# A decay attention with gated convolution on one Trainium2 core: another order of all pieces, and fixed buffer places

## The chip, the core and the metric

The kernel runs on one core of one Trainium2 chip. The metric is the time of one execution on the device, in microseconds (us); lower is better. A core has TensorE (PE, with its weight loads, PEld), VectorE (DVE), ScalarE (ACT), GpSimd (POOL) and SyncE (SP, which here issues all the DMAs). Each engine works through its own instructions in order; they meet at semaphores.

## What is computed

Two layers in a row, in float32, for 4 sequences of 768 tokens, 8 heads of 64 columns. The first is attention with an exponential decay per head, in blocks with a running state; the second gates its output with the sigmoid of a causal convolution over 5 tokens and projects twice:

```python
intra = np.einsum('bhic,bhjc->bhij', qb, kb) * Dmask[None]
intra = np.einsum('bhij,bhjd->bhid', intra, vb)
inter = np.einsum('bhid,bhde->bhie', qb * lam_pow[None], kv_state)
out[:, :, sl] = intra + inter
kb_dec = kb * rev_pow[None]
kv_state = lam_block * kv_state + np.einsum('bhsd,bhse->bhde', kb_dec, vb)
# second layer, x is the attention's output with the heads side by side
gate_pre += conv_w[k][None, None, :] * xp[:, k:k + S, :]      # k = 0..4
gate = 1.0 / (1.0 + np.exp(-gate_pre))
return (gate * (x @ w_val)) @ w_out
```

The weights `w_val`, `conv_w` and `w_out` come as float64, the rest as float32.

## The kernel before

The work is cut into 12 items: a pair of sequences times six chunks of 128 tokens. Items 0 to 5 belong to the first pair, 6 to 11 to the second. All work is a list of 695 named pieces, each with an engine, the pieces it needs, and a function that emits its instructions; `plan.add` collects them. A table, `ORDER`, lists all names once. `Plan.run` (line 101) walks the table and emits each piece, so a piece stands on its engine in the order of the table. No scheduler changes that.

The pieces, with i the item, b the sequence of the pair, u a half of the columns or heads:

- SP: `ld.i.0` and `ld.i.2` load the two halves (1 MB each) of an item; `wv.u`, `wo.u` load halves of the two weights (1 MB each), `cv` the convolution's; `o.i.b.j` stores.
- Weights: `wv.u.k.*`, `wo.u.k.*`, `cv.*` make float32 out of the float64 bits: `e`, `w`, `s`, `v` on VectorE (lines 241 to 270), `m`, `r` on ScalarE; then `h` rounds to a high part on ScalarE (276) and `l` subtracts to a low part on POOL (280). `dm`, `dc`, `qe` make the decay masks.
- Attention on TensorE: `s` scores (431, 441; items 0 to 2 are done in "big" form, whole chunks of 128, in two halves), `ia` scores times v (496, 481), `in` the state's part (507, 518), `st` the state's update (535, 543). Around it: `m` masks on VectorE (454, 461), `up` adds the state there (550, 552), `fd` fades it on POOL (555), `kd` scales k on ScalarE or POOL (378, 381), `qd` scales q on POOL (390, 397).
- Between the layers: `x` copies the result for the convolution (605), `hi` its history, `xh` and `xl` split it into a high part (ScalarE, 627, 629) and a low part (`x_lo`; VectorE for items 0 and 1, 635, else POOL, 639).
- Second layer: `v.i.f` is a quarter of x @ w_val (line 704, twelve matmuls of 256 columns: high by high, low by high, high by low); `t.n.c.k` are the five taps (663 on ScalarE, 665 on VectorE), `sg` the sigmoid, for units of two items; `pb` copies v out of PSUM for items 0 to 5, `ap` gates (718), `hh` and `hl` split again (741, 744); `p.i.b.j.u` is the output projection (767, six matmuls of 512 columns for each u), `ev` evicts (774).

Buffers come from pools by a tag and a rotation (`SLOTS`): a piece that takes a tag gets the next of its places in turn and waits for that place's last reader. PSUM has one place for the big scores (`s`), one for the attention's result (`xp`) and four places `u` that all the rest shares: half of the big scores, states, `v`, taps, `p`, weights. SBUF has three places for loads (`ld`), two for scaled q (`qd`), three for x, two for stores (`o`), and so on.

Of the kernel before, what the change touches and what calls it, by code (L numbers as in the profile page):

```python
# [37 lines left out]
cv.e cv.m wv.1.1.r cv.r st.1 hi.0 xl.1 x.1 v.0.0 up.1.0 v.0.1 wv.1.1.s wv.1.1.v v.1.0 pb.0.0 v.1.1 m.2.1.0 ld.4.2 cv.s
fd.1.0 cv.w wo.0.1.s cv.v wo.0.0.r wo.0.0.s wo.0.0.m wo.0.0.w wo.0.0.v wv.1.1.h ld.4.0 wv.1.1.l qd.4.1 ld.2.2 s.4.0
qd.4.0 ia.2.0 wo.1 t.0.3.0 t.0.3.1 wo.0.1.m wo.0.1.w wo.0.1.v wo.0.0.h t.0.3.2 t.0.3.3 t.0.3.4 m.4.1.0 pb.1.0 ia.2.1  # L40
m.4.0.0 kd.2 t.0.2.0 t.0.0.0 t.0.0.1 t.0.2.1 t.0.2.2 t.0.2.3 t.0.2.4 v.1.2 v.1.3 wo.0.1.h pb.1.1 qd.2.0 in.2.0 x.2
ld.3.0 s.3.0 v.0.2 wo.0.0.l m.3.0.0 wo.0.1.l sg.0.3 xh.2 qd.3.0 qd.3.1 st.2 up.2.0 ld.3.2 kd.3 hi.1 m.3.1.0 sg.0.2
t.0.0.2 t.0.0.3 t.0.0.4 v.0.3 wo.1.1.e pb.0.1 xl.2 kd.4 ia.3.0 st.3 in.3.0 ld.7.0 v.2.0 fd.2.0 up.3.0 fd.3.0 sg.0.0
wo.1.1.r wo.1.1.s ap.1.1 in.3.1 up.3.1 fd.3.1 wo.1.1.m wo.1.1.w wo.1.1.v ia.3.1 x.3 xh.3 xl.3 v.2.1 pb.2.0 ia.4.0 st.4
wo.1.1.h wo.1.1.l ld.5.0 in.4.0 up.4.0 fd.4.0 t.0.1.0 t.0.1.1 v.2.2 v.2.3 pb.2.1 t.0.1.2 t.0.1.3 t.0.1.4 sg.0.1
wo.1.0.e wo.1.0.r v.3.0 in.4.1 ia.4.1 ap.0.1 ap.0.0 v.3.2 ap.1.0 wo.1.0.s wo.1.0.m wo.1.0.w wo.1.0.v s.5.0 x.4 hi.2
qd.5.1 v.3.1 hh.1.0 hl.1.0 up.4.1 m.5.0.0 xh.4 xl.4 wo.1.0.h m.5.1.0 t.1.1.0 t.1.1.1 ld.6.0 t.1.3.0 t.1.3.1 t.1.3.2
# [781 lines left out]
```

## Time and profile before

| | |
|---|---|
| timed runs, median of 3 | 214.48 us (214.25 to 215.65) |
| profiled execution, first to last instruction (span) | 211.9 us |
| TensorE busy in it | 201.8 us, 95% |
| VectorE, ScalarE, POOL busy | 156.2, 114.6, 114.4 us |
| DMA moved | 36.17 MB, 171 GB/s on average |

The profile is of one execution; no time of it but its span was recorded, so the span is set beside the median of the timed runs. A row of a timeline gives the start, the length, the engine, the line, the operation, what it writes and reads, and how often; in brackets stands the idle time of the engine just before, with what ended it. Matmuls are pipelined: their lengths overlap, and the step from one start to the next tells what one costs. A float32 matmul shows as two.

### The profile page before, as it was taken

How to read it: one execution, taken by the hardware profiler on the slowest of the kernel's cores; microseconds unless marked ns; L12 is line 12 of the kernel's file. 1: busy time of each engine (PE TensorE's matmuls, PEld its weight loads, DVE VectorE, ACT ScalarE, POOL GpSimd, SP SyncE). 2: the span in 40 equal slices, each digit the busy share in tenths (PEclk: the TensorE clock that was granted, in tenths of full speed). 3: DMA queues.
4: the chain of work that ended last, by engine and by line, in shares of the span. 5: the costliest groups of instructions: out<-in, count | busy, mean ns of one | idle time of the engine just before them, and what ended most of it. 6: DMA issues, size and time to landing. Idle time of an engine off the chain costs nothing.

```text
span 211.9 us, 7763 instructions
## 1 busy us (share of the span) xinstructions
PE 201.8 (95%) x3460; PEld 179.7 (85%) x3460; DVE 156.2 (74%) x240; ACT 114.6 (54%) x218; POOL 114.4 (54%) x103
## 2 busy tenths in 40 slices
PE   8767899999999999999999999999999999999994
PEld 7457798999998879898888889889899889999883
DVE  5899899997899996999699768786635787432200
ACT  2455698899385884754744563840413582511411
POOL 5139459965949583969796847299400440400000
PEclk9999999999999999999999999999999999999999
DMA  5999999154268057194841099320100112010223
GB/s 194 421 422 425 425 425 421 59 198 113 97 223 373 6 192 257 47 340 170 264 184 54 22 316 309 159 99 6 48 5 3 50 50 104 0 50 3 99 87 111
DMA packets 7953, 36.17 MB, mean 171 GB/s; under 512 B 1136, under 2 KB 1392, under 8 KB 4336
## 3 DMA queue, kind: packets, MB, share of 16 engines
q1 hardware_dynamic: 7920, 35.68, 44.9%
q8 instruction: 27, 0.44, 0.8%
q14 instruction: 6, 0.05, 0.1%
HBM read 29.38 MB, written 6.29 MB: 168 GB/s over the span
## 4 chain that ended last, share of the span: by engine, by line
PE 61%; DVE 15%; DMA 8%; POOL 6%; issue 5%; ACT 2%; SPq 2%; ACTq 0%; DVEq 0%; POOLq 0%
PE op L767 26%; PE vp L704 23%; DMA ld<-in_qkv 8%; DVE acc L665 6%; PE xp L481 3%; PE xp L518 3%; PE st L543 3%; POOL x_lo L639 2%; PE s L441 2%; POOL qd L397 2%; DVE w_em L258 1%; DVE g L718 1%; DVE w_em L241 1%; ACT ld L378 1%; DVE A L454 1%
## 5 line engine op out<-in xcount | busy, mean ns | idle before, releaser
L665 DVE SCALAR_TENSOR_TENSOR acc<-x,conv_sb,acc 128x512 f32<-128x512 f32 x96 | 71.3, 754 | 6.5 <-ACT acc L663 4.3
L767 PE MATMUL op<-wo_hi,hs 128*128 128x512 f32 (+1 forms) x200 | 61.4, 390 | 0.6 <-ACT val L713 0.3
L704 PE MATMUL vp<-x_hi,wv_hi 128*128 128x256 f32 x192 | 55.8, 291 | 0.3 <-DVE w_em L270 0.3
L704 PE MATMUL vp<-x_lo,wv_hi 128*128 128x256 f32 x192 | 54.4, 283 | 0.1
L704 PE MATMUL vp<-x_hi,wv_lo 128*128 128x256 f32 x192 | 54.3, 283 | 0.0
L767 PEld LDWEIGHTS op<-wo_hi,hs 128*128 128x128 f32 x200 | 36.1, 188 | 8.5 <-issue 0.7
L767 PE MATMUL op<-wo_lo,hs 128*128 128x512 f32 (+1 forms) x100 | 38.5, 385 | 0.0
L704 PEld LDWEIGHTS vp<-x_hi,wv_hi 128*128 128x128 f32 x192 | 36.7, 191 | 1.6 <-issue 0.5
L639 POOL TENSOR_TENSOR x_lo<-x,x_hi 128x1024 fp32r<-128x1024 f32 x10 | 23.9, 2399 | 25.2 <-ACT x_hi L629 25.2
L704 PEld LDWEIGHTS vp<-x_lo,wv_hi 128*128 128x128 f32 x192 | 36.8, 191 | 0.5 <-POOL x_lo L639 0.3
L704 PEld LDWEIGHTS vp<-x_hi,wv_lo 128*128 128x128 f32 x192 | 36.8, 191 | 0.0
L774 ACT COPY o<-op 128x512 f32<-128x512 f32 (+1 forms) x25 | 14.2, 569 | 29.0 <-PE op L767 23.4
L397 POOL TENSOR_TENSOR qd<-ld,qdec_c 128x512 f32<-128x512 f32 (+1 forms) x18 | 22.3, 1253 | 3.6 <-PE xp L518 3.6
L555 POOL TENSOR_TENSOR sdec<-state,qdec_c 128x512 f32<-128x512 f32 x17 | 18.4, 1085 | 7.9 <-DVE state L552 7.9
L670 ACT ACTIVATE g<-acc 128x512 f32<-128x512 f32 x24 | 14.3, 597 | 15.1 <-DVE acc L665 15.1
L767 PEld LDWEIGHTS op<-wo_lo,hs 128*128 128x128 f32 x100 | 18.8, 188 | 4.0
L744 POOL TENSOR_TENSOR hs<-g,hs 128x512 fp32r<-128x512 f32 x12 | 15.4, 1298 | 12.2 <-ACT hs L741 12.2
L552 DVE TENSOR_TENSOR state<-st,sdec 128x512 f32<-128x512 f32 x17 | 11.7, 687 | 11.3 <-PE st L543 8.0
L605 ACT COPY x<-xp 128x512 f32<-128x512 f32 x24 | 12.9, 591 | 9.3 <-PE xp L481 7.3
L741 ACT CAST hs<-vp 128x512 fp32r<-128x512 f32 x12 | 7.0, 590 | 18.2 <-DVE vp L718 18.2
L663 ACT ACTIVATE acc<-x,conv_sb 128x512 f32<-128x512 f32 x24 | 16.2, 689 | 0.6
L381 POOL TENSOR_TENSOR ld<-ld,dmask 128x512 f32<-128x512 f32 x12 | 12.9, 1106 | 5.3 <-DMA ld<-in_qkv 5.3
(71 smaller groups left out, 290.7 us busy)
## 6 DMA issues: line engine op xcount, KB each, us to landing
ld<-in_qkv SPq DMA_DIRECT2D x24, 1024.0 KB, 7.7
out<-o SPq DMA_DIRECT2D x23, 256.0 KB, 2.0
w_raw<-in_w_val SPq DMA_DIRECT2D x2, 1024.0 KB, 8.0
w_raw<-in_w_out SPq DMA_DIRECT2D x2, 1024.0 KB, 18.7
out<-o SPq DMA_DIRECT2D x2, 128.0 KB, 1.7
conv_raw<-in_conv_w SPq DMA_DIRECT2D x1, 20.0 KB, 18.6
lam_bc<-in_lam SPq DMA_DIRECT2D x1, 4.0 KB, 1.7
```

Of the source, the lines that this page charges most:

```text
L381: nc.gpsimd.tensor_tensor(out=kv[:, b], in0=kv[:, b], in1=k_mask.to_broadcast([P, H, D]), op=ALU.mult)
L397: nc.gpsimd.tensor_tensor(out=s["qd"][:, hs, ms], in0=lds[i]["qT"][:, u].rearrange("p h (m i) -> p h m i", m=2)[:, :, ms], in1=qdec[:, hs, ...
L555: nc.gpsimd.tensor_tensor(out=sdec, in0=state, in1=qdec_c[:, :, n - 1 : n].to_broadcast([P, H, D]), op=ALU.mult)
L605: nc.scalar.copy(*blocks(s["x"], b))
L639: nc.gpsimd.tensor_tensor(out=s["x_lo"], in0=s["x"], in1=s["x_hi"].bitcast(F32), op=ALU.subtract)
L663: nc.scalar.mul(to, src, w)
L665: nc.vector.scalar_tensor_tensor(out=to, in0=src, scalar=w, in1=to, op0=ALU.mult, op1=ALU.add)
L670: nc.scalar.activation(xu[un]["g"][:, ct].rearrange("p u (b i) -> p b u i", b=NB2), xu[un]["acc", ct].rearrange("p b (u i) -> p b u i", u= ...
L704: nc.tensor.matmul(s["vp", u][:, f, :], w[:, ct, fs], xx[:, ct, :], start=n_mm == 0, stop=n_mm == 3 * NT - 1,)
L744: (nc.vector if h_in else nc.gpsimd).tensor_tensor(out=s["h_lo"][:, us], in0=s["h", u], in1=s["h_hi"][:, us].bitcast(F32), op=ALU.subtract,)
L767: nc.tensor.matmul(s["op", b, j][:, cols], hh[:, ft, ts], w[:, ft, cols], start=ft == 0 and n == 0, stop=ft == NT - 1 and n == 2,)
L774: nc.scalar.copy(s["o", b, j][:, cols], s["op", b, j][:, cols])
```

## The change

The table `ORDER` is replaced by another order of the same 695 pieces. Behind a piece that takes a buffer the table now also names the place it takes (`v.0.0:u1`), so places no longer rotate: each is a pool tag of its own with one buffer. `Plan.slot` hands the place to the piece. Nothing else is changed; the pieces and their needs are the same.

```diff
 ORDER = """
-f.0 f.1 wv.0 dm.0 qe dm.1 ld.0.0 wv.0.1.e wv.0.0.e ld.0.2 wv.1 wv.0.0.m wv.0.1.m wv.0.0.w wv.0.1.w wv.0.0.r kd.0
...
+wv.0:g0 ld.0.0:ld0 ld.0.2 qe dm.1 wv.1:g1 ld.1.0:ld1 ld.1.2 ld.2.0:ld2 f.0:u0 dm.0 f.1:u0 wv.0.0.e:val0 f.2:u0
...
 """
+    def slot(self, tag):
+
+        return self.takes.pop(next(n for n, t in enumerate(self.takes) if t.rstrip("0123456789") == tag))
+
     def run(self):
         done = set()
-        for name in ORDER.split():
+        for piece in ORDER.split():
+            name, _, takes = piece.partition(":")
             k = self.at[name]
             assert k not in done and done.issuperset(self.work[k][3]), name
             done.add(k)
+            self.takes = takes.split(",") if takes else []
             self.work[k][2]()
+            assert not self.takes, piece
...
     def buf(tag, name, shape, dt=F32):
-        return work.tile(shape, dt, name=name, tag=tag, bufs=SLOTS[tag])
+        return work.tile(shape, dt, name=name, tag=plan.slot(tag), bufs=1)

     def bank(name, shape, tag="u"):
-        return psum.tile(shape, F32, name=name, tag=tag, bufs=SLOTS[tag])
+        return psum.tile(shape, F32, name=name, tag=plan.slot(tag), bufs=1)
...
-    warm = bank("warm", [P, C])
+    warm = psum.tile([P, C], F32, name="warm", tag="u0", bufs=1)
...
-            s["x_hi"] = work.tile([P, NT, NB2, C], F32R, name="x_hi", bufs=SLOTS["xs"])
-            s["x_lo"] = work.tile([P, NT, NB2, C], F32R, name="x_lo", bufs=SLOTS["xs"])
+            at = plan.slot("xs")
+            s["x_hi"] = work.tile([P, NT, NB2, C], F32R, name="x_hi", tag=f"{at}_hi", bufs=1)
+            s["x_lo"] = work.tile([P, NT, NB2, C], F32R, name="x_lo", tag=f"{at}_lo", bufs=1)
```

On SP, at the program's start, the loads stand thus before (an `ld` number is an item's buffer: 123 is item 0, 216 item 1, 235 item 2, 442 item 4; `w_raw` are the weights):

```order
L332 DMA w_raw_105<-in_w_val 128x2048
L314 DMA ld_123<-in_qkv 128x2048 x2
L332 DMA w_raw_132<-in_w_val 128x2048
L314 DMA ld_216<-in_qkv 128x2048
L314 DMA ld_235<-in_qkv 128x2048
L314 DMA ld_216<-in_qkv 128x2048
L332 DMA w_raw_343<-in_w_out 128x2048
L347 DMA conv_raw_95<-in_conv_w 128x40
L314 DMA ld_442<-in_qkv 128x2048 x2
```

and after the change (103 is item 0, 120 item 1, 123 item 2, 231 item 4):

```order
L347 DMA w_raw_101<-in_w_val 128x2048
L329 DMA ld_103<-in_qkv 128x2048 x2
L347 DMA w_raw_118<-in_w_val 128x2048
L329 DMA ld_120<-in_qkv 128x2048 x2
L329 DMA ld_123<-in_qkv 128x2048
L329 DMA ld_231<-in_qkv 128x2048
L329 DMA ld_123<-in_qkv 128x2048
L347 DMA w_raw_244<-in_w_out 128x2048
L329 DMA ld_231<-in_qkv 128x2048
L362 DMA conv_raw_95<-in_conv_w 128x40
```

The second half of item 1 now comes ahead of the first of item 2; the first half of `w_out` moves behind a half of item 4 and the second of item 2, and `conv_w` behind the second half of item 4.

On TensorE, from its first scores on, before (`s` and `so` are the two score halves of one item, `xp` the attention's result, `st` the state):

```order
L431 MATMUL s<-ld 128x128 x8
L431 MATMUL so<-ld 128x128 x8
L496 MATMUL xp<-A,ld 64x128 x16
L535 MATMUL st<-ld 64x64 x16
L431 MATMUL so<-ld 128x128 x8
L431 MATMUL s<-ld 128x128 x8
L431 MATMUL so<-ld 128x128 x8
L431 MATMUL s<-ld 128x128 x8
L496 MATMUL xp<-A,ld 64x128 x16
L507 MATMUL xp<-qd,state 64x128 x16
L535 MATMUL st<-ld 64x64 x16
L704 MATMUL vp<-x_hi,wv_hi 128x256
```

and after the change:

```order
L446 MATMUL s<-ld 128x128 x8
L446 MATMUL so<-ld 128x128 x8
L511 MATMUL xp<-A,ld 64x128 x16
L550 MATMUL st<-ld 64x64 x16
L446 MATMUL s<-ld 128x128 x8
L446 MATMUL so<-ld 128x128 x8
L720 MATMUL vp<-x_hi,wv_hi 128x256
```

The first quarter `v.0.0` now stands ahead of item 1's `ia`; the scores of item 2, `st.1` and item 4's scores follow between the other quarters.

On POOL, right behind the decay table `qe`, before:

```order
L381 TENSOR_TENSOR ld<-ld,mask_c 128x512 x2
L390 TENSOR_TENSOR qd<-ld,qdec_c 128x512
L280 TENSOR_TENSOR wv_lo<-w_em,wv_hi 128x4x128 x2
L555 TENSOR_TENSOR sdec<-state,qdec_c 128x512
L390 TENSOR_TENSOR qd<-ld,qdec_c 128x512 x2
L280 TENSOR_TENSOR wv_lo<-w_em,wv_hi 128x4x128
```

and after the change:

```order
L295 TENSOR_TENSOR wv_lo<-w_em,wv_hi 128x4x128
L396 TENSOR_TENSOR ld<-ld,mask_c 128x512 x2
L295 TENSOR_TENSOR wv_lo<-w_em,wv_hi 128x4x128
L405 TENSOR_TENSOR qd<-ld,qdec_c 128x512 x3
L570 TENSOR_TENSOR sdec<-state,qdec_c 128x512
L295 TENSOR_TENSOR wv_lo<-w_em,wv_hi 128x4x128
```

The low part of the first weight quarter now stands ahead of `kd.0` (`ld<-ld,mask_c`), and three `qd` ahead of the first fade.

## Rows read from the trace of the kernel before

**Rows 1.** The page: busy time by engine, two costly POOL groups, the instruction queue.

```profile
PE 201.8 (95%) x3460; PEld 179.7 (85%) x3460; DVE 156.2 (74%) x240; ACT 114.6 (54%) x218; POOL 114.4 (54%) x103
...
q8 instruction: 27, 0.44, 0.8%
...
L397 POOL TENSOR_TENSOR qd<-ld,qdec_c 128x512 f32<-128x512 f32 (+1 forms) x18 | 22.3, 1253 | 3.6 <-PE xp L518 3.6
...
L555 POOL TENSOR_TENSOR sdec<-state,qdec_c 128x512 f32<-128x512 f32 x17 | 18.4, 1085 | 7.9 <-DVE state L552 7.9
```

**Rows 2.** Two stretches: length, busy time by engine, granted clock, DMA share, GB/s.

```profile
26.25:208.80 182.55, 181.54 (x3184) 162.88 (x3180) 133.60 (x195) 100.93 (x191) 100.71 (x81) 1.00 0.39 142
208.80:211.90 3.10, 0.00 (x0) 0.00 (x0) 0.00 (x0) 0.37 (x1) 0.00 (x0) 1.00 0.35 127
```

**Rows 3.** Timeline of TensorE at the start: start us, us, what, [idle before].

```profile
8.66 1.16 PE L431 MATMUL s<-ld 64*128 64x128 f32 x16 [1.11 <-DMA ld<-in_qkv]
...
11.26 1.26 PE L496 MATMUL xp<-A,ld 128*64 128x128 f32 x16 [0.55 <-DMA ld<-in_qkv]
13.44 1.09 PE L496 MATMUL xp<-A,ld 128*64 128x128 f32 x16 [0.92 <-DVE A L454]
...
16.11 1.16 PE L431 MATMUL so<-ld 64*128 64x128 f32 x16 [0.65 <-DMA ld<-in_qkv]
17.08 1.09 PE L431 MATMUL s<-ld 64*128 64x128 f32 x16
...
22.24 1.97 PE L496 MATMUL xp<-A,ld 128*64 128x128 f32 x32 [0.70 <-DMA ld<-in_qkv]
24.14 1.10 PE L507 MATMUL xp<-qd,state 64*64 64x128 f32 x32
...
26.25 0.38 PE L704 MATMUL vp<-x_hi,wv_hi 128*128 128x256 f32 x1
```

**Rows 4.** Timeline of TensorE at its later waits.

```profile
35.52 0.36 PE L704 MATMUL vp<-x_hi,wv_hi 128*128 128x256 f32 x1 [0.27 <-DVE w_em L270]
...
65.06 0.73 PE L767 MATMUL op<-wo_hi,hs 128*128 128x512 f32 x2 [0.34 <-ACT val L713]
...
79.40 0.70 PE L767 MATMUL op<-wo_hi,hs 128*128 128x512 f32 x2 [0.28 <-DVE state L550]
...
143.87 0.38 PE L704 MATMUL vp<-x_hi,wv_hi 128*128 128x256 f32 x1
144.37 0.38 PE L704 MATMUL vp<-x_lo,wv_hi 128*128 128x256 f32 x1
```

**Rows 5.** The chain that ended last: start us, us, what.

```profile
4.33 17.77 DMA ld<-in_qkv
...
46.96 1.63 PE vp L704 x12
...
84.01 0.47 PE xp L518 x32
...
174.72 14.39 PE vp L704 x120
```

**Rows 6.** Timeline of VectorE: a pair of masks, the start on w_out.

```profile
18.96 1.28 DVE L454 TENSOR_TENSOR A<-s,mask_c 128x512 f32<-128x512 f32 x2
...
24.68 0.43 DVE L241 TENSOR_SCALAR w_em<-w_raw 128x512 int32<-128x512 int32 x1
```

**Rows 7.** Timeline of POOL: `kd.0`, then two low parts of weights.

```profile
11.26 2.07 POOL L381 TENSOR_TENSOR ld<-ld,mask_c 128x512 f32<-128x512 f32 x2 [5.03 <-DMA ld<-in_qkv]
...
17.34 2.51 POOL L280 TENSOR_TENSOR wv_lo<-w_em,wv_hi 128x512 fp32r<-128x512 f32 x2
```

**Rows 8.** Timeline of ScalarE: the high part of item 0.

```profile
15.27 1.07 ACT L627 CAST x_hi<-xp 128x512 fp32r<-128x512 f32 x2
```

**Rows 9.** Line 718: duration ns min/median/max, first and last start us.

```profile
L718 DVE TENSOR_TENSOR g<-val,g x12: 676/689/1616, 49.8 to 116.1; 128x512 f32<-128x512 f32 x12
```

**Rows 10.** Groups of VectorE, shapes apart: busy us, mean ns, idle before.

```profile
L718 DVE TENSOR_TENSOR g<-val,g 128x512 f32<-128x512 f32 x12 | 11.7, 1000 | 0.8 <-ACT g L670 0.8
```

More of the change, by code (lines that the diff above doesn't have):

```diff
@@ L38 @@
[L38 to L47, printed above, removed]
@@ new lines @@
+wv.0.1.e:val1 wv.0.0.m:u1 wv.0.0.r wv.0.0.w wv.0.1.r wv.0.0.s s.0.0:s0 dc wv.0.0.v wv.0.1.s s.0.1:u0,u2 wv.0.1.m:u3
+m.0.0.0:A0 wv.0.0.h m.0.0.1:A1 wv.0.0.l m.0.1.0 m.0.1.1 kd.0 ia.0.0:xp0 wv.0.1.w ia.0.1 wv.0.1.v wv.1.1.e:val2
+xh.0:xs0 st.0:u1 wv.1.0.e:val3 wv.0.1.h xl.0 ld.4.0:ld0 wv.0.1.l ld.2.2 s.1.0:s0 wo.0:hs0 up.0.0 x.0:x0 s.1.1:u0,u2
+ld.4.2 qd.1.1:qd0 m.1.0.0:A0 cv wv.1.0.m:u3 m.1.1.0 v.0.0:u1 wv.1.1.r qd.1.0 m.1.1.1:A1 wv.1.0.r m.1.0.1 ia.1.0:xp0
+wv.1.1.s wv.1.1.m:u0 wv.1.0.s kd.1 ia.1.1 wv.1.0.w in.1.0 wv.1.0.v qd.2.1:qd1 wv.1.1.w v.0.1 wv.1.0.h wv.1.1.v fd.0.0
@@ new lines @@
+s.2.0:s0 pb.0.0:val0 wv.1.0.l xh.1:xs1 s.2.1:u2,u3 wv.1.1.h qd.4.1:qd0 v.0.2:u0 m.2.1.1:A0 m.2.0.0:A1 qd.2.0 kd.2
+m.2.1.0 st.1:u1 xl.1 wv.1.1.l s.4.0:s0 ld.3.0:ld1 ld.3.2 m.2.0.1 x.1 qd.4.0 v.0.3 wo.0.1.e:val1 hi.0 ia.2.0:xp0 up.1.0
+wo.0.1.m:u2 ia.2.1 cv.e fd.1.0 m.4.0.0:A1 cv.m wo.0.1.r st.2:u3 wo.0.0.e:val3 in.2.0 m.4.1.0 ld.5.0:ld2 wo.0.0.r
+wo.1:hs1 cv.w wo.0.1.s wo.0.0.m:u1 s.3.0:s0 qd.3.1:qd1 x.2:x1 up.2.0 v.1.0:u3 m.3.0.0:A0 cv.r pb.0.1 fd.2.0 cv.s kd.3
+v.1.1 qd.3.0 wo.0.1.w wo.0.1.v ia.3.0:xp0 wo.0.0.s xh.2:xs0 in.3.0 cv.v wo.0.0.w st.3:u0,u2 pb.1.0:val2 wo.0.0.v xl.2
@@ new lines @@
+wo.0.1.h v.1.2:u3 up.3.0 t.0.0.0:u1,g0 kd.4 t.0.0.1 v.1.3 t.0.0.2 wo.0.1.l m.3.1.0 in.3.1 hi.1 t.0.0.3 t.0.3.0:u0
+fd.3.0 s.5.0:s0 pb.1.1 t.0.3.1 qd.5.1:qd1 wo.0.0.h ia.3.1 up.3.1 v.2.2:u3 x.3 ld.6.0:ld1 t.0.0.4 ld.5.2 fd.3.1
+wo.1.1.e:val1 ld.6.2 xh.3:xs1 v.2.3 wo.0.0.l sg.0.0 t.0.3.2 wo.1.1.r ia.4.0:xp0 t.0.3.3 st.4:u2,u1 xl.3 pb.2.1:val3
+m.5.1.0:A0 t.0.3.4 in.4.0 v.2.0:u3 sg.0.3 up.4.0 wo.1.1.m:u0 wo.1.1.s fd.4.0 t.0.1.0:u2 in.4.1 wo.1.1.w ia.4.1 t.0.1.1
+v.2.1 qd.5.0 x.4:x2 ld.7.0:ld0 wo.1.1.v t.0.1.2 wo.1.1.h kd.5 v.3.0:u0 t.0.1.3 xh.4:xs0 up.4.1 pb.2.0 v.3.1 t.0.1.4
@@ new lines @@
+t.0.2.0:u1 fd.4.1 m.5.0.0 sg.0.1 t.0.2.1 kd.6 wo.1.1.l st.5:u3 t.0.2.2 ia.5.0:xp0 xl.4 t.0.2.3 in.5.0 v.3.2:u2 up.5.0
+t.0.2.4 v.3.3 ap.1.0 sg.0.2 wo.1.0.e:val1 ap.1.1 wo.1.0.m:u3 s.6.0:s0 hh.1.0:hs0 wo.1.0.w in.5.1 pb.3.1:val2 hl.1.0
+m.6.1.0:A1 ia.5.1 wo.1.0.r v.4.2:u1 x.5 ld.9.0:ld2 wo.1.0.s qd.7.0:qd0 ld.7.2 m.6.0.0 t.1.3.0:u2,g1 v.4.3 wo.1.0.v
+ap.0.0 wo.1.0.h pb.3.0 ap.0.1 s.7.0:s0 wo.1.0.l hh.1.1 t.1.3.1 pb.4.1:val0 ia.6.0:xp0 t.1.3.2 st.6:u3,u0 hl.1.1
+t.1.3.3 p.1.1.0.0:u1 up.6.0 qd.6.0:qd1 t.1.3.4 t.1.2.0:u3 fd.6.0 p.1.1.0.1 sg.1.3 t.1.2.1 qd.6.1 t.1.2.2 p.1.0.0.0:u2
@@ new lines @@
+v.5.0:u3 ev.0.1.0:o0 t.2.2.3 hh.3.0:hs1 o.0.1.0 t.2.2.4 o.1.0.0 hh.2.1 hl.3.0 v.5.2:u1 ld.10.2:ld0 t.2.0.2 sg.2.2
+t.2.1.0:u0 t.2.0.3 kd.9 v.5.3 hh.3.1 t.2.0.4 t.2.1.1 sg.2.0 v.5.1 hl.2.1 t.2.1.2 t.2.1.3 p.2.1.0.0:u2 kd.8 pb.5.0:val1
+pb.5.1 t.2.1.4 t.2.3.0:u3 p.2.1.0.1 t.2.3.1 qd.8.0 t.2.3.2 p.2.0.0.0:u1 ev.2.1.0:o0 fd.7.1 t.2.3.3 p.2.0.0.1
+m.8.0.0:A1 qd.9.0:qd0 t.2.3.4 m.8.1.0 sg.2.3 ia.8.0:xp0 hl.3.1 ev.2.0.0:o1 in.8.0 sg.2.1 st.8:u2,u3 o.2.0.0 hi.3
+ld.10.0 ap.4.0 o.2.1.0 p.3.1.0.0:u1 ap.4.1 hh.4.0:hs0 ap.5.0 t.3.2.0:u0,g1 hl.4.0 up.8.0 p.3.1.0.1 ap.5.1 fd.8.0
@@ new lines @@
+in.8.1 ev.3.1.0:o1 t.3.2.1 ia.8.1 s.9.0:s0 x.8:x1 t.3.2.2 ld.11.2:ld1 qd.9.1 p.3.0.0.0:u2 t.3.2.3 hh.4.1 t.3.2.4
+hl.4.1 p.3.0.0.1 up.8.1 sg.3.2 m.9.0.0:A0 t.3.0.0:u1 kd.10 t.3.0.1 st.9:u3,u0 hh.5.1:hs1 ev.3.0.0:o0 t.3.0.2
+ia.9.0:xp0 xh.6:xs0 o.3.0.0 fd.8.1 in.9.0 t.3.0.3 p.4.1.0.0:u2 hh.5.0 up.9.0 m.9.1.0 t.3.3.0:u3 fd.9.0 p.4.1.0.1
+t.3.3.1 hl.5.0 t.3.0.4 s.10.0:s0 sg.3.0 hl.5.1 in.9.1 ev.4.1.0:o0 m.10.0.0:A1 ia.9.1 o.4.1.0 t.3.3.2 hi.4 ld.11.0
+p.4.0.0.0:u1 xl.6 x.9 o.3.1.0 t.3.3.3 t.4.1.0:u2,g0 up.9.1 p.4.0.0.1 xh.7:xs1 t.4.1.1 fd.9.1 t.3.3.4 p.5.0.0.0:u0
@@ new lines @@
+t.4.1.2 qd.10.0:qd1 sg.3.3 ev.4.0.0:o0 t.4.1.3 p.5.0.0.1 t.3.1.0:u3 qd.10.1 t.4.1.4 v.6.2:u1 t.3.1.1 ev.5.0.0:o1
+m.10.1.0 sg.4.1 o.5.0.0 t.3.1.2 ia.10.0:xp0 st.10:u0,u2 t.3.1.3 t.3.1.4 in.10.0 v.6.3 sg.3.1 up.10.0 fd.10.0 v.6.0:u3
+ap.6.1 qd.11.0:qd0 hh.6.1:hs0 v.6.1 t.4.0.0:u0 hl.6.1 kd.11 t.4.0.1 s.11.0:s0 ap.6.0 t.4.0.2 xl.7 hh.6.0 in.10.1
+ia.10.1 m.11.0.0:A0 p.5.1.0.0:u1 hl.6.0 x.10:x2 t.4.0.3 t.4.2.0:u3 up.10.1 p.5.1.0.1 t.4.2.1 fd.10.1 t.4.2.2 v.7.2:u2
+ev.5.1.0:o1 qd.11.1 t.4.2.3 o.5.1.0 v.7.3 t.4.2.4 sg.4.2 xh.9:xs0 ia.11.0:xp0 st.11:u1 xl.9 in.11.0 v.7.0:u3 up.11.0
@@ new lines @@
+m.11.1.0 ap.7.1 hi.5 v.7.1 t.4.0.4 hh.7.1:hs1 in.11.1 ap.7.0 ia.11.1 hh.7.0 p.6.1.0.0:u1 sg.4.0 hl.7.0 t.4.3.0:u0
+p.6.1.0.1 xh.8:xs1 t.4.3.1 hl.7.1 xl.8 p.6.0.0.0:u3 t.4.3.2 ev.6.1.0:o1 o.6.1.0 t.4.3.3 p.7.1.0.0:u2 t.4.3.4 sg.4.3
+p.7.1.0.1 x.11 v.8.0:u1 ev.7.1.0:o1 t.5.3.0:u0,g1 o.7.1.0 o.4.0.0 v.8.1 t.5.3.1 p.6.0.0.1 ap.8.0 t.5.3.2 v.8.2:u2
+ev.6.0.0:o1 hh.8.0:hs0 t.5.0.0:u3 hl.8.0 v.8.3 t.5.3.3 t.5.0.1 v.9.0:u1 xh.10:xs1 t.5.3.4 ap.8.1 sg.5.3 v.9.1 t.5.0.2
+hh.8.1 hl.8.1 p.7.0.0.0:u0 t.5.0.3 t.5.0.4 p.7.0.0.1 ap.9.0 sg.5.0 v.9.2:u2 ev.7.0.0:o0 hh.9.0:hs1 o.7.0.0 t.5.1.0:u3
@@ new lines @@
+o.6.0.0 hl.9.0 v.9.3 t.5.2.0:u0 p.8.1.0.0:u1 xh.11:xs0 ap.9.1 hh.9.1 xl.11 p.8.1.0.1 hl.9.1 t.5.1.1 p.8.0.0.0:u2
+ev.8.1.0:o0 t.5.2.1 xl.10 t.5.2.2 p.8.0.0.1 t.5.1.2 t.5.1.3 p.9.1.0.0:u1 ev.8.0.0:o1 t.5.2.3 o.8.0.0 o.8.1.0 t.5.2.4
+p.9.1.0.1 t.5.1.4 sg.5.2 p.9.0.0.0:u2 p.9.0.0.1 v.10.2:u0 ev.9.0.0:o1 sg.5.1 o.9.0.0 v.10.3 v.10.0:u2 v.10.1 v.11.2:u3
+ap.10.0 hh.10.0:hs0 v.11.3 ev.9.1.0:o0 hl.10.0 o.9.1.0 v.11.0:u1 ap.11.1 hh.11.1:hs1 v.11.1 hl.11.1 ap.10.1
+p.10.0.0.0:u2 hh.10.1 ap.11.0 hl.10.1 hh.11.0 p.10.1.0.0:u3 hl.11.0 p.11.1.0.0:u0 p.11.1.0.1 p.10.1.0.1 ev.11.1.0:o1
@@ L78 @@
+o.11.1.0 p.11.0.0.0:u1 ev.10.1.0:o0 o.10.1.0 p.10.0.0.1 p.11.0.0.1 ev.10.0.0:o1 o.10.0.0 p.11.1.1.0:u0 ev.11.0.0:o0
+p.11.1.1.1 o.11.0.0 ev.11.1.1:o1 o.11.1.1
 """
@@ L141, in decay_attention_then_gated_conv @@
     psum = ctx.enter_context(tc.tile_pool(name="psum", bufs=1, space=PSUM))
+    plan = Plan()
+    add = plan.add
     def buf(tag, name, shape, dt=F32):
[L144 removed]
+        return work.tile(shape, dt, name=name, tag=plan.slot(tag), bufs=1)
     def bank(name, shape, tag="u"):
[L147 removed]
+        return psum.tile(shape, F32, name=name, tag=plan.slot(tag), bufs=1)
     ctx.enter_context(tc.manual_schedule())
```

41 lines of the change are left out of this document (5 added, 36 removed).

## The prediction

> **What bounds the kernel now.** I read the engines' busy shares first [rows 1]: TensorE is busy for 201.8 us of the span of 211.9 us, VectorE for 74% of it. Two stretches say where the rest lies [rows 2]: from 26.25 to 208.80 us TensorE is busy for 181.54 of 182.55 us, at a granted clock of 1.00 (2.4 GHz), and behind it come 3.1 us of the last eviction and its store. So the span is the time until TensorE runs without gaps (26.25 us), its work, and the tail. The work is the same in any order. What an order can change is idle time of TensorE, and there are two stocks of it.
>
> The first is the start [rows 3]. TensorE's first real piece begins at 8.66 us when `ld.0.0` lands, and up to 26.25 us it waits for loads and for VectorE's masks; four of those waits stand in the rows (0.55, 0.92, 0.65 and 0.70 us). A row's idle time leaves out that a matmul's last 0.16 us or so overlap the next one, so I take the steps from start to start where nothing waits: 0.97 us for one half of the big scores (16.11 to 17.08), 0.95 for a half of the big `ia` (22.24 to 24.14), 1.05 for a big `in` or `st` (two between 24.14 and 26.25). Six score halves, four `ia` halves, one `in` and two `st` are 12.8 us of work in those 17.6 us: 4.8 us are idle. The second stock is single waits later [rows 4]: about 0.4 us before 35.52 (a weight product of VectorE late), 0.5 before 65.06 and 0.4 before 79.40 (a PSUM place not yet read), and 0.4 between 143.87 and 144.37, where the second matmul of `v.7.0`, the first with `x_lo`, starts 0.5 us after the first instead of 0.12. With the shorter ones (0.15 us in the `in.10.0` ahead of 143.87) this stock is 1.9 us.
>
> **The change, part by part.** *Places of buffers* cost nothing themselves: no piece of work is added or removed, and each waits for the last reader of its place as before. *Switches:* a block of small matmuls between two of the big ones costs TensorE time: twelve `v` matmuls alone need 1.44 us (14.39 us for 120), entered from small ones 1.63 [rows 5]. The old order has 22 such blocks of small pieces, the new 23. The extra one lies in the walk below.
>
> *The start.* I walk the new order with the rows' durations. Loads land one after the other, about a MB every 2.5 us: `ld.0.0` at 8.6, `ld.0.2` 11.2, `ld.1.0` 16.0 [rows 3], `ld.1.2` (then 7th) at 22.1 [rows 5], the first half of `w_out` (8th) by 24.7, when VectorE starts on it [rows 6]. New: `ld.1.2` is 6th, 18.5 to 19.7; `ld.2.0` 7th, by 22.1; `ld.4.0` by 24.6; `ld.2.2` by 27.1; `w_out` 10th, 28.5 to 29.5; `conv_w` behind `ld.4.2`, 31 to 32.
>
> - VectorE makes `wv.0.0` (three steps, and one of `wv.0.1`) before the masks, at 0.6 us a step (two in 1.28 less the overlap [rows 6]): the masks end at 12.2 and 12.7, `ia.0` runs 12.2 to 14.1. POOL takes `wv.0.0.l` (1.26 us) ahead of `kd.0` (2.07) [rows 7], so `st.0` waits until 14.9; `s.1` 16.0 to 17.95.
> - `x_hi` of item 0 (1.07 us on ScalarE [rows 8]) ends at 15.4, VectorE's `x_lo` at 16.8: `v.0.0` starts at 18.0, eight microseconds before its old start, in time that stood idle for `ld.1.2`.
> - `ia.1`, `in.1.0` 19.75 to 22.6; `v.0.1` to 24.15; `s.2` to 26.2; `v.0.2` to 27.8. POOL has `wv.1.0.l` by 25.7: three `qd` at 1.25 and an `fd` at 1.09 [rows 1], the third `qd` held for `ld.2.0` until 22.1. Half a microsecond of margin.
> - `st.1`, `s.4.0`, `v.0.3` to 31.4; `ia.2`, `st.2`, `in.2.0` to 35.45; `s.3.0` to 36.4. `v.1.0` needs place u3, which `up.2.0` frees at 36.1. `v.1.0` to `ia.3.1` then end at 46.7 without a wait.
>
> At that point the old order (49.6, the next start after its `ia.3.1`, reached from 26.25 by the same steps) had done `v.2.0` too (1.44 us) and not yet `s.5.0` (0.93): at equal work the new order is 49.6 − 0.5 − 46.7 = 2.4 us ahead, its extra switch paid. I take **−2.4 us**. Bounds: of the 4.8 us the new order still spends 1.6 before `ia.0` and 0.8 before `st.0`, so 2.4 is about the most; the least is 0.4, if loads land 2 us after my upper ends.
>
> *The later waits.* For each PSUM place I looked where its last reader stands in its queue. At a dozen places of the new order the reader ends 0.3 to 1 us before TensorE wants the place (`v.1.2`, `v.2.2`, `p.1.0.0.0`, `v.4.0` among them), at none after it. Bounds: nothing waits (−1.9), or as much as before (0). With so many small margins some will be missed: I take 0.8 us of waits, **−1.1 us**.
>
> *Instruction pages.* TensorE's 2 × 3460 instructions come in 27 fetches of 0.44 MB together [rows 1]: about 128 matmuls with their weight loads each, which 64-column matmuls pass in 4 × 0.47 = 1.9 us [rows 5]. The longest block of those, 192 of them before 143.87, lost 0.15 us; the longest of the new order has 160. So pages can give 0.15 us a block at most, and no other row shows it; I count nothing. The Trainium skill ("Runtime: NRT & Kernel Launch", section "Instruction fetch mechanics") says that the next block is fetched while the current one runs and that a crossing is mostly hidden: by that rule pages give 0.0, and an order made to respect them spends its freedom on nothing. The trace agrees so far.
>
> *The tail.* The last piece is the same half-width `p` with one eviction and one store: 3.1 us again [rows 2]. The last `hl` is ready some 0.6 us before TensorE asks for it.
>
> Sum: 211.9 − 2.4 − 1.1 = 208.4 us of span. The profiled execution's span is 2.6 us under the median of the timed runs (214.48); I keep that around it: **211.0 us**.
>
> **Rivals.**
> - *`w_out` comes too late for VectorE* (chance 0.17). Two loads are moved ahead of it. VectorE reaches `wo.0.1.e` at 27.9 and waits until 29.5, then for `conv_w` from 30.9 until 32.1; before, `w_out` was there when VectorE came to it. For it: those 2.8 us, and `up.2.0`, which ends only 0.3 us before `v.1.0` wants u3. Against: by the same walk VectorE is 1.3 us early at `in.4.1`, 1.6 at `ia.5.0`, and more behind. Loads later by 1.5 to 3.3 us than my upper ends delay TensorE by 1.2 to 3.0: 212.2 to 214.0 us.
> - *The change doesn't do what it says* (0.17). If it was aimed at page stalls, there are none to take; if an early wait that I don't see eats the start too, what is left is the 1.1 us of later waits or nothing: 213.4 to 214.5.
> - *VectorE and POOL block each other, slower than before* (0.08). The twelve gating products with both operands in SBUF take 0.68 us at least and 1.62 at most [rows 9], 1.00 on average [rows 10]. The new order puts POOL's `kd`, `hl` and `qd` beside other ones of them. If all twelve took the most, that is 12 × 0.62 = 7.4 us more; VectorE's margin is about 1.5, so TensorE would lose 5.9 after a gain of 3.5: 216.9. Slower by over 1% needs eleven of the twelve blocked, or taps with them. The Trainium skill ("SBUF — State Buffer", section "Who interferes with whom") makes it a lock: the shared port pair goes to whichever starts first, for its whole instruction. The spread agrees; it speaks against any order made on fixed durations.
>
> **How the numbers follow.** My case (0.58): 209.2 to 212.2, all faster by over 1% (under 212.3; 1% is about what a measurement of this kernel can tell from no change). Of the first rival a quarter ends under 212.3 (0.04); its rest and the second lie within 1% (0.30); the last is slower (0.08). Range: low is every later wait gone and a little in my steps, 209.0; high takes in the first rival and some of the second, 214.2.
>
> **What the new profile would show.** Right: the first `vp` matmul near 18 us, TensorE without gaps from about 20 us, `ia.3.1` over near 46.7, waits after that under 1 us together, the last matmul near 205.3. The start is wrong if TensorE waits for VectorE or POOL at a `vp` between 26 and 37 us; the loads if VectorE's `w_em<-w_raw` of `w_out` starts after 31; the waits if `op` or `vp` rows show PSUM readers at over 0.5 us each. A slower kernel would show `g<-val,g` well over 1 us on average.

## The result, and the profile after

| | before | after |
|---|---|---|
| timed, median of 20 | 214.21 us (213.70 to 215.65) | 214.09 us (210.54 to 217.81) |
| ratio, 95% interval | | 0.990 (0.988 to 0.993) |
| profiled execution | span 211.9 us | span 208.8 us, 210.54 us in all |

The ratio counts the executions within 1.5% of their kernel's fastest: all 20 before, but only 9 after, since the other 11 run to 217.8 us with a granted clock of about 0.99, and over all 20 the medians are equal. So the change is 1% faster in half of its executions and gives next to nothing on the whole. What the other half loses became the main question, which the prediction had not asked.

The page of the profiled execution (busy time by engine, the instruction queue), against [rows 1]:

```profile
PE 201.3 (96%) x3460; PEld 179.7 (86%) x3460; DVE 155.1 (74%) x240; ACT 115.2 (55%) x218; POOL 115.0 (55%) x103
...
q8 instruction: 27, 0.44, 0.9%
```

Two stretches (length, busy time by engine, granted clock, DMA share, GB/s), against [rows 2]:

```profile
26.25:205.70 179.45, 178.18 (x3194) 160.80 (x3190) 133.38 (x199) 99.61 (x187) 99.79 (x80) 1.00 0.40 144
205.70:208.80 3.10, 0.00 (x0) 0.00 (x0) 0.00 (x0) 0.37 (x1) 0.00 (x0) 1.00 0.35 127
```

The work and the tail are unchanged: 201.3 us busy, 3.1 us behind the last matmul, which ends at 205.69 instead of 208.80. TensorE's timeline (start us, us, what, [idle before]), against [rows 3, 4]:

```profile
12.37 1.75 PE L511 MATMUL xp<-A,ld 128*64 128x128 f32 x28 [0.63 <-DVE A L469]
...
14.93 1.15 PE L550 MATMUL st<-ld 128*64 128x64 f32 x30 [0.69 <-POOL ld L396]
...
18.13 0.39 PE L720 MATMUL vp<-x_hi,wv_hi 128*128 128x256 f32 x1
...
36.92 1.16 PE L456 MATMUL s<-ld 64*64 64x64 f32 x64 [1.11 <-DMA ld<-in_qkv]
...
43.30 0.39 PE L720 MATMUL vp<-x_hi,wv_hi 128*128 128x256 f32 x1 [0.15 <-ACT val L729]
```

`v.0.0` starts at 18.13 us instead of 26.25, in time that had been idle. One large wait is left, and the prediction's walk had not seen it: 1.11 us ahead of `s.3.0`, for item 3's load. Behind 43.30 us no wait is left at all; the four of [rows 4] are gone. VectorE's timeline around the second weight, and the gating product (duration ns min/median/max), against [rows 6, 9]:

```profile
30.19 0.97 DVE L256 TENSOR_SCALAR w_em<-w_raw 128x512 int32<-128x512 int32 x1
...
32.16 0.18 DVE L256 TENSOR_SCALAR w_em<-conv_raw 128x20 int32<-128x20 int32 x1
```

```profile
L734 DVE TENSOR_TENSOR g<-val,g x12: 675/685/1187, 64.3 to 108.5; 128x512 f32<-128x512 f32 x12
```

Neither row waits noticeably for its load, and the gating products became shorter: 0.77 us on average.

### The profile page after: what moved, and what is told of

The parts are those of the page before. It is cut to its first block, busy times and chain, and to the rows that moved or that the text cites. A ratio compares the mean times of both kernels' runs of the same rounds, so it can differ in the third digit from the quotient of the medians.

```text
span 208.8 us, 7746 instructions
## 1 busy us (share of the span) xinstructions
PE 201.3 (96%) x3460; PEld 179.7 (86%) x3460; DVE 155.1 (74%) x240; ACT 115.2 (55%) x218; POOL 115.0 (55%) x103
## 4 chain that ended last, share of the span: by engine, by line
PE 78%; DMA 13%; POOL 3%; ACT 2%; SPq 2%; issue 1%; ACTq 0%
PE op L783 33%; PE vp L720 30%; DMA ld<-in_qkv 13%; PE xp L496 4%; PE xp L533 4%; PE st L558 4%; PE s L456 4%; POOL qd L405 1%; ACT ld L393 1%; SPq L329 1%; POOL wv_lo L295 1%; POOL qd L412 1%; SPq L347 1%; POOL sdec L570 0%; ACT x_hi L645 0%
## 5 line engine op out<-in xcount | busy, mean ns | idle before, releaser
L655 POOL TENSOR_TENSOR x_lo<-x,x_hi 128x1024 fp32r<-128x1024 f32 x10 | 24.5, 2461 | 29.2 <-ACT x_hi L645 29.2
L720 PEld LDWEIGHTS vp<-x_hi,wv_hi 128*128 128x128 f32 x192 | 36.4, 190 | 1.8 <-ACT val L729 0.3
L720 PEld LDWEIGHTS vp<-x_lo,wv_hi 128*128 128x128 f32 x192 | 36.4, 190 | 0.3
L720 PEld LDWEIGHTS vp<-x_hi,wv_lo 128*128 128x128 f32 x192 | 36.4, 190 | 0.0
L570 POOL TENSOR_TENSOR sdec<-state,qdec_c 128x512 f32<-128x512 f32 x17 | 19.0, 1117 | 9.1 <-DVE state L567 9.1
L734 DVE TENSOR_TENSOR vp<-vp,g 128x512 f32<-128x512 f32 x12 | 8.4, 697 | 13.4 <-PE vp L720 13.4
```

Of the source, the lines that this page charges most:

```text
L570: nc.gpsimd.tensor_tensor(out=sdec, in0=state, in1=qdec_c[:, :, n - 1 : n].to_broadcast([P, H, D]), op=ALU.mult)
L655: nc.gpsimd.tensor_tensor(out=s["x_lo"], in0=s["x"], in1=s["x_hi"].bitcast(F32), op=ALU.subtract)
L720: nc.tensor.matmul(s["vp", u][:, f, :], w[:, ct, fs], xx[:, ct, :], start=n_mm == 0, stop=n_mm == 3 * NT - 1,)
```

## The experiments

Spans below are of single executions; a timed execution lies 1.7 to 1.85 us above its span. The clock given for an execution is its mean granted clock; in round brackets stand the lowest and highest time and the number of executions. Behind many runs stands what the kernel before or the changed kernel took when it was measured beside them.

**The changed kernel again, twice** (no edit).

> The changed kernel once more, unchanged, for its spread from execution to execution and a second profile. Theory L (a late load): the start gained only part of the 2.4 us forecast because the scores of item 3 (s.3.0) wait 1.1 us at 35.8 us for ld.3.0, which SP could issue only at 29.37 us, when st.1 had freed its place; L expects the same wait again, between 0.5 and 3 us, and the executions to differ by what it measures (spans 208.5 to 213). Theory C (the clock alone): the wait is the same to 0.1 us in every profile, and the executions differ only by the granted clock.

> The changed kernel once more, beside the two shifts on the same chip: spans from 207 to 213.5 us again, about half of the executions with a granted clock near 0.99.

Measured: 212.06 us (208.92 to 215.26, 6 executions) and 213.85 us (210.86 to 217.42, 12). Of 38 executions of this kernel, with the first 20, 20 had a clock under 0.995, with spans from 211.8 to 216.0; the other 18 ran from 207.1 to 213.5. The kernel before, measured beside these and later runs, had such a clock in 14 of 69. The median over all 38 is 213.85 us, over the 69 it is 214.04. Both new profiles were of executions with the low clock, and they show the same place. TensorE's timeline in the first:

```profile
51.58 0.33 PE L533 MATMUL xp<-qd,state 64*64 64x64 f32 x9
54.39 0.81 PE L533 MATMUL xp<-qd,state 64*64 64x64 f32 x20 [2.47 <-issue]
```

Stretches of it (columns as above):

```profile
51.70:54.40 2.70, 0.23 (x16) 0.15 (x8) 0.66 (x1) 1.20 (x2) 0.18 (x1) 1.00 1.02 422
54.40:57.80 3.40, 3.40 (x35) 3.28 (x34) 2.37 (x4) 0.69 (x1) 1.60 (x2) 0.50 0.50 210
```

In the middle of `in.4.0`, between two matmuls that need nothing new, TensorE stops for 2.69 us from start to start; "issue" means that the profile shows nothing it waited for. Behind it the clock stands at 0.50 (1.2 GHz) for 3.4 us, another 1.7 us of work. Together 4.4 us in this execution. The second profile has a stop of 2.97 us there and the same fall of the clock, and one of 0.92 us at 47.45 as well. That the other executions with a low clock stopped at this place is inferred from their clock; their median span is 213.3 us, against 210.55 for the rest. And the 1.11 us ahead of `s.3.0` is not there in either profile. Theory L was half right (a wait that comes and goes), theory C wrong in that the wait does change.

What else happened there: the instruction queue. In the first profile from 46.7 to 52.1 us (packets, MB, share):

```profile
q1 hardware_dynamic: 200, 1.51, 79.6%
```

and from 52.1 to 53.1:

```profile
q1 hardware_dynamic: 49, 0.40, 98.0%
q8 instruction: 1, 0.02, 5.5%
```

No instructions are fetched for 5.4 us, while 1.5 MB of loads pass; then one block of 16 KB, and 1.4 us after its end TensorE goes on. In the profile of the result the fetch of that block falls between 48.4 and 50.7, a stretch in which only 0.25 MB of loads pass:

```profile
q1 hardware_dynamic: 30, 0.25, 49.2%
q8 instruction: 1, 0.02, 2.6%
```

The stop is behind the 985th of TensorE's 3460 matmuls in both profiles. 27 fetches for 3460 matmuls, as many weight loads and some 40 waits make about 256 instructions a block. Counted through with all of these, this stop and every other one behind 28 us that a trace puts down to "issue", 29 in the ten traces that have any, stand at the same instruction of a period of 256, to within one: at the boundary between two blocks. This became **theory P**: TensorE stops at a boundary when the next block's fetch comes late.

**`st.1` earlier.**

```diff
-v.0.2:u0 m.2.1.1:A0 m.2.0.0:A1 qd.2.0 kd.2 m.2.1.0 st.1:u1 xl.1
+st.1:u1 v.0.2:u0 m.2.1.1:A0 m.2.0.0:A1 qd.2.0 kd.2 m.2.1.0 xl.1
```

> The changed kernel with one piece moved: st.1, the last reader of item 1's load place, stands ahead of v.0.2 instead of behind it (1.6 us earlier on TensorE), so that ld.3.0 can be issued at about 27.7 us. Theory L: the wait of 1.1 us before s.3.0 goes, nothing else waits, span 208.8 - 1.1 = 207.7 us, about 1.1 us under the unchanged order in the same call, and a narrower spread. Theory C, or a queue that is full anyway: ld.3.0 lands at the same 36.8 us whenever it is issued, the wait stays, and the time is the same within 0.2 us.

Measured: 215.43 us (213.09 to 218.67, 12 executions), slower than the changed kernel beside it (212.06); 9 of 12 with a clock near 0.99. TensorE's timeline:

```profile
36.06 1.13 PE L456 MATMUL s<-ld 64*64 64x64 f32 x64
...
41.63 0.28 PE L496 MATMUL xp<-A,ld 64*64 64x64 f32 x3 [0.79 <-issue]
...
55.95 0.57 PE L533 MATMUL xp<-qd,state 64*64 64x64 f32 x22 [2.69 <-issue]
```

The wait for the load is gone, as L said, but it is gone in both repetitions too, so that the earlier issue removed it isn't shown. TensorE now stops at two block boundaries, 1.0 and 2.9 us from start to start. The first of them does not come of the missing wait alone: in the first repetition the wait is missing as well, and that boundary passes without a stop. Call TensorE's step into a new block a crossing. There the fetch behind the crossing before this boundary starts 0.9 us after it; here, with the loads moved, some 3.5 us after it, at 39.27.

**Places alone, order alone.** The new order in the old code (names without places, pools of several buffers), and the old order in the new code, each place fixed as it had been:

```diff
-        return self.takes.pop(next(n for n, t in enumerate(self.takes) if t.rstrip("0123456789") == tag))
+        self.turn[tag] = self.turn.get(tag, -1) + 1
+        return f"{tag}{PLACES[tag][self.turn[tag]]}"
```

> The new order of pieces in the old code, with the pools choosing the places: all SBUF places come out the same as in the changed kernel, PSUM places of the group u differ. If fixed places cost and bring nothing (the prediction's step): the same as the changed kernel within 0.3 us, 208.5 to 209.5 us of span. If the fixed PSUM places are what removed the later waits: one to four waits of 0.2 to 0.5 us for a PSUM reader at vp or op rows after 48 us, and 0.5 to 1.5 us slower.

> The old order with each buffer place fixed to the one that it had in the kernel before: the other half of the change by itself. If places cost nothing: span 211.9 us as before, ratio 1.000 within 0.002, the same four later waits (35.5, 65.1, 79.4, 144 us) and idle start. If one pool tag per place changes the waits that are set: some of the later waits go or new ones come, 0.4 us or more each. Its executions also show whether the granted clock of the old order ever falls under 1.00.

Measured: 211.17 us (209.30 to 215.24, 7) for the new order with pools; its profile stops behind the same 985th matmul for 2.69 us, and has two waits of 0.2 us behind 48 us where the changed kernel has none. 213.55 us (213.35 to 213.99, 12) for the old order with fixed places, 0.4 us under the kernel before beside it and with less spread, though every place is the same; why stays open. The gain and the stops belong to the order, not to the places. The places also corrected the text ahead of the prediction: in the old code they don't come strictly in turn. The PSUM group `u` went 3, 2, 1, 0, 3, 2, 3, 1.

**Block boundaries moved**, nothing else: tiny products of zeros among the warm-up, ahead of the first load.

```diff
-WARM = 9
+WARM = 7
+SHIFT = 30
...
+    for n in range(SHIFT):
+        b, m = slice(n % 2 * D, n % 2 * D + D), slice(n // 2 % 2 * D, n // 2 % 2 * D + D)
+        nc.tensor.matmul((warm, warm2)[n % 2][m, :D], zero[b, :D], zero[b, :D], start=True, stop=True)
```

> The changed kernel with 112 more TensorE instructions ahead of everything (two warm-up products fewer, 30 tiny products of zeros more, done before the first load is there), so that the same order stands 112 instructions later in TensorE's blocks of 256. Theory P (pages): where one block of 256 passes in some 2 us, the fetch of a later one is missed, TensorE stands 2.7 us for it and its clock falls to 1.2 GHz for 3.4 us, 4.4 us together. Counted in the trace of the changed kernel, unshifted blocks take 2.08, 2.23 and 3.17 us at the least; shifted by 112, none takes under 3.4. P expects no such stall in any execution, spans 207 to 209.5 us, granted clock 0.998 or more, the median about 2 us under the unchanged kernel's 212 to 214. Rival C (the clock falls for a reason of its own): half the executions at 0.99 as before, spans to 213.5.

> The same with 176 more instructions (46 tiny products): by the same count blocks of 1.86 us (from 71.2), 2.19 us (82.9) and 2.58 us (114.4). P expects a stall of about 2.7 us, seen as a gap inside a piece with no releaser and a late instruction fetch, behind at least the first in every execution, perhaps behind all three; spans 212 to 222 us, no execution under 211. Rival C: as unshifted, 207 to 213.5 us.

> The old order with fixed places (which ran at 213.4 to 214.0 us), its blocks shifted by 192 instructions (50 tiny products): blocks of 1.83 us (82.8), 1.99 (102.0) and 1.85 (141.1), two of them inside small matmuls from end to end, instead of 1.99, 2.24 and 2.39 that each begin right behind large matmuls. P expects stalls here too, behind one to three of these places, 3 to 13 us slower than the old order. If only the new order has a cause of stalls of its own (its places, its loads at 50 us): no stall, 213.5 us.

Measured: 216.90 us (215.01 to 219.15, 12), 220.70 (217.48 to 223.81, 4), and for the old order 225.24 (221.83 to 225.77, 4). These kernels also come to `v.0.0` 0.4 to 1.7 us later than unshifted; most of the rest is stops. By 112:

```profile
39.56 0.34 PE L461 MATMUL s<-ld 64*64 64x64 f32 x5 [1.66 <-issue]
...
60.15 0.56 PE L501 MATMUL xp<-A,ld 64*64 64x64 f32 x22 [1.75 <-issue]
```

By 176:

```profile
78.15 0.50 PE L563 MATMUL st<-ld 64*64 64x64 f32 x17 [2.38 <-issue]
```

The old order by 192, and a stretch of it:

```profile
88.42 0.33 PE L506 MATMUL xp<-A,ld 64*64 64x64 f32 x4 [2.11 <-issue]
...
111.50 0.80 PE L506 MATMUL xp<-A,ld 64*64 64x64 f32 x18 [3.39 <-issue]
```

```profile
111.50:114.60 3.10, 3.10 (x30) 2.98 (x31) 0.69 (x1) 2.06 (x4) 3.10 (x4) 0.50 0.43 90
```

That boundaries decide is shown: the same matmuls in the same order, up to 12 us slower by 50 tiny products that are done before the data is there, and the old order, whose three unshifted profiles show no stop, has them too. As the cause of these stops rival C is out: by 112 two of them pass at a clock of 1.00. What it says of the clock is not settled for the old order: there the 14 executions with a low clock lie only 1.35 us over the others (medians 213.45 and 212.1), less than one stop of 2.7 us, and none of them was profiled. Where TensorE stops, theory P forecast in part: the largest stops of the old order, and the one at 75.5 by 176, stand behind short blocks that it had named. But it named none for 112, and there TensorE stopped behind blocks of 3.2 and 3.6 us, with loads running (323 GB/s in the stop at 37.7). The shortest block is not the rule.

**Many small matmuls where nothing is loaded.**

```diff
-                for k in range(W_S):
+                for k in [*range(W_S)] * (8 if i == 11 else 1):
```

> The changed kernel with the scores of item 11 done eight times over (the same results into the same place), at about 135 us, where few loads run: 512 small matmuls in a row, four blocks of instructions. If pages cost nothing (the prediction's step, and the rule that a crossing is mostly hidden): 7 x 0.93 = 6.5 us more. Under P each block of 1.9 us has to wait for a fetch, two to four stalls of 1 to 2.7 us and a fall of the clock: 10 to 18 us more.

Measured: one execution, 227.14 us, with the stop behind the 985th matmul (3.24 us) and 6.8 us of half clock, which begin 1 us before that stop ends. The eightfold piece itself:

```profile
145.15 2.09 PE L456 MATMUL s<-ld 64*64 64x64 f32 x128 [1.24 <-issue]
148.88 2.02 PE L456 MATMUL s<-ld 64*64 64x64 f32 x121 [1.63 <-issue]
...
152.61 0.62 PE L533 MATMUL xp<-qd,state 64*64 64x64 f32 x25 [1.63 <-issue]
```

DMA from 139 to 151 us: three fetches, and nothing besides.

```profile
DMA packets 3, 0.05 MB, mean 4 GB/s; under 512 B 0, under 2 KB 0, under 8 KB 0
## 3 DMA queue, kind: packets, MB, share of 16 engines
q8 instruction: 3, 0.05, 1.8%
```

This is the price alone: a block of 128 small matmuls takes 1.87 us, then TensorE stops for 1.46, 1.85 and 1.85 us from start to start, 5.2 us for three boundaries. One block comes every 3.7 us (145.15 to 148.88, 148.88 to 152.61). The step "pages cost nothing" is refuted.

**A shift that theory P2 held to be good.**

```diff
-WARM = 9
+WARM = 2
-        nc.tensor.matmul(warm, zero, zero, start=True, stop=True)
+        nc.tensor.matmul(warm, zero, zero[:, None, :].to_broadcast([P, 4, C]), start=True, stop=True)
```

> The changed kernel with 28 TensorE instructions fewer ahead of everything (two wide warm-up products in place of nine narrow ones), so that the same order stands 28 instructions earlier in the blocks of 256. The shifts by 112 and 176 stalled at other block boundaries than unshifted, and mostly where loads run; so theory P is refined to P2: at the crossing into a block the next one is fetched, and until it can run that takes some 3 us where no loads run (0.6 to the fetch, 1.0 for it, 1.35 until the first matmul) and some 5.4 us where they do; a block that passes faster stalls TensorE at its end by the difference, and a fetch that is missed altogether costs 2.7 us and 3.4 us of half clock. Reckoned over the trace of the changed kernel the smallest margin is 0.2 us unshifted (blocks of 2.2 and 2.1 us from 46.3 and 65.6, each begun behind large matmuls), and 0.6 us shifted by -28. P2 expects no stall of over 1 us in the profile and the granted clock at 0.998 or more in at least two thirds of the executions, spans 207 to 210 us, a median of 209 to 211.5 us. Rival C (the clock falls for a reason of its own): as the unshifted kernel in the same call.

> The same shift by -28 with st.1 ahead of v.0.2 too, which alone was slower since it stalled at two block boundaries (41.6 and 53.0 us). P2: with the boundaries moved, the earlier load gives back what it could not give alone; margins of 0.5 us and more; against the shift alone 0 to 1.1 us faster, by as much as s.3.0 waits there. If st.1 early is bad for another reason (DMA order, ScalarE): 1 us or more slower than the shift alone.

Measured: 220.35 us (214.33 to 222.41, 12 executions) and 219.79 (219.33 to 220.34, 6). P2 failed as a forecast. TensorE's timeline by -28, and a stretch:

```profile
55.45 0.35 PE L533 MATMUL xp<-qd,state 64*64 64x64 f32 x9 [2.10 <-issue]
...
79.65 0.56 PE L558 MATMUL st<-ld 64*64 64x64 f32 x22 [3.19 <-issue]
```

```profile
80.40:83.80 3.40, 3.40 (x16) 2.65 (x10) 3.09 (x5) 1.26 (x2) 2.42 (x3) 0.50 0.03 7
```

With `st.1` early too:

```profile
56.23 0.34 PE L533 MATMUL xp<-qd,state 64*64 64x64 f32 x8 [2.65 <-issue]
...
78.98 0.81 PE L558 MATMUL st<-ld 64*64 64x64 f32 x21 [3.19 <-issue]
```

```profile
56.20:62.00 5.80, 5.78 (x107) 5.51 (x108) 5.26 (x9) 3.27 (x6) 4.52 (x4) 1.00 0.56 198
```

The first of these two stops is 2.87 us from start to start, longer than the first repetition's, and the clock stays at 1.00 behind it; by -28 alone a stop of 2.32 us is followed by 3.4 us at 0.50. So the length of a stop doesn't decide by itself whether the clock falls.

28 instructions, less than a ninth of a block, move the median by 6.5 us. What P2 got right is the end of a stop: in all 29 stops of over 0.5 us at a boundary, in ten traces, TensorE goes on 1.2 to 1.6 us after a fetch ends, and these fetches take 0.9 to 1.3 us. What it got wrong is when the fetch starts. There are as many fetches as crossings. Over the crossings behind 28 us in the traces, those left out whose fetch runs ahead of them, it starts 0.7 us later in the median where no load passes in between (some 100 crossings), and about 3 us later, at the most about 6, where half a MB or more does (some 75); the exact figures depend on which matmul is taken as a block's first. P2 took one figure, 2.4 us more, for all of these. That the fetch stands behind load data in a queue fits this, and the stop behind the 985th matmul: the block before it begins within 0.25 us of the issue of `ld.6.0` in all four profiles of the new order (48.58 and 48.59 us in the profile of the result), so that one may come ahead of the other by chance. But a longer delay also sees more data pass, and no run moved a load away from a crossing: this is argued, not shown.

**One late wait of the old order taken away.** `xl.7` and `xl.8` exchanged on POOL, in the old order with fixed places.

```diff
-p.6.1.0.0 p.6.1.0.1 ev.6.1.0 xl.8 t.4.3.1 xl.7 t.4.3.2
+p.6.1.0.0 p.6.1.0.1 ev.6.1.0 xl.7 t.4.3.1 xl.8 t.4.3.2
```

> The old order with fixed places and one exchange: xl.7 ahead of xl.8 on POOL, so that x_lo of item 7 is there 2.4 us before TensorE asks for it at 143.9 us (in the kernel before the second matmul of v.7.0 waited 0.4 to 0.5 us for it). If a wait in the dense stretch of TensorE comes back one to one: 213.55 - 0.45 = 213.1 us. If something else is as late there (a PSUM place, a page): 213.5 us.

Measured: 213.30 us (212.87 to 214.64, 12), 0.25 us under the old order with fixed places, which was measured at another time. Before the exchange:

```profile
144.40 0.39 PE L725 MATMUL vp<-x_lo,wv_hi 128*128 128x256 f32 x1 [0.28 <-POOL x_lo L660]
```

After it the idle time in brackets is gone there, `v.7.0` takes 1.69 us instead of 2.23 from its first matmul's start to its last one's end, and the last matmul of all ends at 208.28 instead of 208.72 us: 0.44 us, as reckoned. In the timed medians some half of it is seen; the kernel before, measured beside each, came to 213.93 and 213.91.

## Why the prediction was right, and where it was not

**The number.** 211.0 us was forecast for the likeliest case, with faster by over 1% at 0.62. The profiled execution took 210.54 us, the ratio is 0.990, on the line between faster and same; but the median over all executions, 214.1, lies at the upper end of the range, 214.2. In the profiled execution the two parts of the gain are there, but their sizes changed places: the start gave 1.7 us less than forecast, the later waits 1.3 more, and 0.8 us less was to be added from span to time. That 211.0 came within 0.5 us of it is luck in part. The other half of the executions lost time to a cost that was set at nothing.

**The start: forecast -2.4 us; -0.7 in the profiled execution, -2.4 without the late load.** Term by term the walk held: `v.0.0` at 18.1 (18.0 forecast), the big scores of item 2 over at 26.4 (26.2), `in.2.0` at 35.8 (35.45). The step that failed is "`s.3.0` to 36.4": it took item 3's load for granted, and SP could issue that only at 29.4 us, when `st.1` had freed its place; it landed at 36.8, 7.4 us later. So the matmul behind `ia.3.1` started at 48.36, and 49.6 - 0.5 - 48.4 = 0.7 us were won. In the first profile of the repetition SP issued it at 29.2, the loads from there took 5.4 to 7.7 us to land instead of 6.8 to 9.6, and it came in time: the same matmul started at 46.67 us, 2.4 us ahead, against 46.7 forecast. So the late issue left no margin, and the landing decided.

**The later waits: forecast -1.1 us, taken as "some will be missed"; all were avoided.** From `ia.3.1` on, 3.1 - 0.7 = 2.4 us were won. The old order's waits in that part are 1.6 us of it (0.5, 0.4, 0.4 and shorter ones), and the exchange of `xl.7` shows in its profile that such a wait comes back in full. Where the rest, some 0.8 us, comes from stays open. The bound of -1.9 counted waits alone.

**The pages: nothing forecast, which was the wrong step.** [Rows 5] show 128 small matmuls in 1.9 us, and the prediction saw that the longest block of them had lost only 0.15 us. It took the fetches in the page of the profile as a count and never asked when each one starts. In the profiles of the old order no block that passes in 2 us meets a late fetch; that is a property of that order at its offset (the number of instructions ahead of it), as the shift by 192 showed. The Trainium skill ("Runtime: NRT & Kernel Launch", section "Instruction fetch mechanics") has the crossing of a boundary mostly hidden. The measurement differs: 1.5 to 1.9 us a crossing among small matmuls with nothing else on the DMA engines, up to 3.6 us with loads, and 1.7 us more where the clock falls. And the prediction's sentence that an order made to respect pages spends its freedom on nothing had the matter the wrong way round: of the four offsets tried, the one that the new order stands at is the only one at which its median is not above the kernel before's.

**The tail: 3.1 us, as forecast. Span to time: 2.6 us forecast, 1.8 measured** (210.54 - 208.8). The 2.6 set one execution's span against the median of others; one execution's own two numbers are always 1.7 to 1.85 us apart here. With 1.8 the sum would have been 210.2.

**The rivals.** *`w_out` too late* (0.17): did not come about; VectorE came to it at 30.19 us, 2.3 us later than the walk had it, took it without a noticeable wait, and `conv_w` at 32.16. *The change doesn't do what it says* (0.17): over half of the executions ended in its time (213.4 to 214.5) or behind it. The profiles of two of them show stops at page boundaries, of which this rival, too, said that there were none to take. *VectorE and POOL block each other* (0.08): the gating products took 0.77 us on average instead of 1.00.

**Right or wrong in the profile.** The first `vp` matmul near 18 us, the last matmul near 205.3 (205.7) and under 1 us of later waits came true; "without gaps from about 20 us" did not, by the one load.
